# Experts' part of a gated Fourier mix as a sixth contraction chunk of the closing Strassen step

## Chip, cores, metric

One core of a Trainium2 chip runs the whole kernel in one launch. The metric is device time in microseconds, the median of the runs shown; lower is better. A profile comes from one further execution of the same program, with its own time. PE is TensorE, DVE VectorE, ACT ScalarE, POOL GpSimd; SP is the sync engine, whose queue issues most DMAs.

## What is computed

For 2048 tokens of width 640, with x, all in float32:

```python
g = sigmoid((x * gate_w).sum(-1, keepdims=True))
a = Re(DFT_seq(DFT_hidden(x)))          # as products with cos/sin matrices, 2048x2048 and 640x640
# PEER experts: 32 heads, two sets of 16 keys, top 2 of each, top 2 of their 4 sums, 256 experts
act = gelu(einsum("nd,nhkd->nhk", x, u[top_e]))
b = einsum("nhk,nhk,nhkd->nd", softmax(top_s), act, v[top_e])
out = g * a + (1 - g) * b
```

Since there are only 256 experts, b is computed densely: f[e, t] is the sum of the gates that token t gives to expert e, and the expert part is z^T v with z[e, t] = gelu(u x)[e, t] * f[e, t] * (1 - g[t]).

## The kernel before

**Precision.** Every float32 matmul is three fp32r matmuls: each operand is split into a high half (ACT copies it to fp32r, line 123) and a low half (the difference, line 124, on POOL or DVE), and `mm3` (lines 128 to 130) adds high-high, high-low and low-high into one PSUM bank. Nearly every operand passes through this chain: a DMA on SP's queue, ACT's copy, POOL's or DVE's difference, three matmuls on PE.

**Stages.** 128 "pieces" (`seq_piece`, five mm3 each, one per 128 output rows) multiply x with the sequence matrices; in between, background work is spread by a credit pump (`bg`): keys and scores, top-2 picks on DVE, and from about 400 us on the `experts` generator, which builds one-hot tables on DVE (L639), multiplies them in bursts of 64x64 matmuls (L650, 16 per table), masks the PSUM result on ACT (L609) and sums it on DVE (L615) into f. The result of the pieces, multiplied by g (L193), is stored to DRAM as the tiles pd[w, c][k]: real or imaginary part w, 512 tokens c, and 128 of the 640 hidden rows k.

**Last part.** `step(m)` forms, for each half b of the tokens, out^T = D_re^T pd[0] + D_im^T pd[1] + v^T z as 2x2 blocks: block rows of the left operand are the half's two token quarters, block columns the real and imaginary part, and the right operand's block columns are output rows 0 to 255 and 256 to 511. Strassen's method (Winograd's form) does this with seven products, the units a11, a12, s1, s2, s4, s3, a22, each over KD = 5 chunks k of 128 hidden rows. A step in a11, a12, s1 and a22 is three mm3 (two output tiles and the fifth output tile "W", rows 512 to 639, which is done plainly), in s2, s4 and s3 two. The operands s1 to s4 are sums of a11 to a22: for half 0 they are made in an earlier stage and stored (pqs), for half 1 they are summed on DVE (L800). The right operand's sums lie in TS (made by `make_sums` and `split_sums`, L738 to L742), its plain blocks in DD.

**Experts in the last part.** `load_z` (L860 to L866) loads for one quarter g, the activations and the gate sums f (four 128x128 DMAs for each of two chunks of 128 experts); `split_z` makes 1 - g (L876), multiplies twice (L879, L880) and splits into `zop`. `z_group` then multiplies with v, outside Strassen: at the end of a12 and the start of a22 (six mm3 each), at the end of s4 and behind s3 (`quarter`, four each), 20 mm3 for each half. At the very end, `very_last` holds back the second output tile's five mm3 of a22 so that the first one can be stored meanwhile.

**Order.** `at(n, f)` queues f behind piece or step n (step m counts as NPC + m, NPC = 128); loads come some steps ahead, the split of step m + 5 is emitted in step m, and each engine works through its own queue strictly in that order, waiting on semaphores. Buffers come from tags: `take` hands a raw tile to a load, `give` returns it once its split is emitted, and SP's queue stands still when the tile at its head is not free. Splits go through a ring of six (four WS, two WP).

Of the kernel before, what the change touches and what calls it, by code (L numbers as in the profile page):

```python
# [16 lines left out]
P = 128  # L17
# [19 lines left out]
NSTEP = 7 * KD  # L37
# [54 lines left out]
def gated_mix_kernel(ctx: ExitStack, tc: tile.TileContext, xT, xn, dreT, dimT, wsre, wsim, wq, kT, uT, vv, gw, out):  # L92
# [43 lines left out]
    gdr = dram.tile([S], F32, name="gdr")  # L136
# [11 lines left out]
    zc, gt, gc = (const.tile([P, 32], F32, name=t) for t in ("zc", "gt", "gc"))  # L148
    nc.gpsimd.memset(zc, 0.0)
# [246 lines left out]
    def gate():  # L396
        nc.scalar.activation(gt, zc, AF.Sigmoid)
        nc.vector.transpose(gc, gt)

    def store_gate():  # L400
        for j in range(4):
            nc.scalar.dma_start(gdr.rearrange("(i j p) -> j i p", j=4, p=32)[j], gc[32 * j:32 * j + NT])
# [191 lines left out]
    HOT = []  # L594

    def experts():
# [45 lines left out]
        def use(group):  # L642
            while masked or unmasked:
                yield settle(True)
            for i, (g, c, s) in enumerate(group):
                t = bank((6, 7, 5)[i], (P, 8, E * 4))
                pt, qt = (HOT[s // 2][:, s % 2, n].rearrange("p (m c) -> p m c", m=16) for n in range(2))
                for m in range(16):
                    r = slice(64 * (m % 2), 64 * (m % 2) + 64)
                    nc.tensor.matmul(t[r, m // 2, :], pt[:, m], qt[:, m], start=True, stop=True)  # L650
                unmasked.append((g, c, t))
                free_sets.append(s)
            yield 0.0
# [24 lines left out]
        assert not last_part  # L678
# [45 lines left out]
    def t_sum(k, n, a):  # L724

        if n < 2:
            return TS[k][:, (2 * n + a) * 2 * P:][:, :2 * P]
        if n == 2:
            return TS[5 + k // 2][:, (2 * (k % 2) + a) * 2 * P:][:, :2 * P]
        return DD[:, 0, a, k, 2 * P:4 * P] if n == 3 else TS[k][:, PAIR + a * P:][:, :P]  # L730

    def make_sums(k):
        if k == 0:
            T["t"] = big.tile([P, 9 * P], F32, name="tf", tag="xl")
# [10 lines left out]
    def split_sums(k):  # L745
        for n in [k] + ([5 + k // 2] if k % 2 == 0 else []):
# [7 lines left out]
    def load_v():  # L754
        T["f"] = big.tile([P, 2, D], F32, name="dt", tag="xf")
        nc.sync.dma_start(T["f"], vv.rearrange("k p d -> p k d"))

    def split_v():
# [7 lines left out]
    def v_neg(a):  # L766
        return TS[5 + a][:, PAIR:].rearrange("p (k d) -> p k d", k=2)
# [5 lines left out]
    at(NPC - 3, load_v)  # L773
    at(NPC, split_v)
    at(NPC + 28, store_gates, 1)


    fresh, raw_free, raw_tags = deque(), deque(), [("wf", 1)] * 5 + [(f"X{s}", 2) for s in range(10, 16)] + [("xf", 2)]
    raw, sp = {}, {}

    def take(key):
        if not fresh and raw_tags:
# [3 lines left out]
            else:  # L786
                r = big.tile([P, 2, TC], F32, name="ra", tag=t)
                fresh.extend(r[:, a] for a in range(2))
# [53 lines left out]
    def split_step(m):  # L842
        if m < 2 * NSTEP:
            b, (u, k) = m // NSTEP, divmod(m % NSTEP, KD)
            what = UNITS[u]
            key = (b, "s" if b and what in ("s1", "s2", "s4") else what, k)
# [3 lines left out]
            if b == 0 or what in ("a11", "a12", "a22", "s3", "s4"):  # L850
                give(key)

    zop = {}

    def load_z(b, n):
# [4 lines left out]
        nc.sync.dma_start(take((b, "g", n)), gdr[c * TC:(c + 1) * TC].partition_broadcast(P))  # L860
        for k in range(2):
            a, f = take((b, "za", k)), take((b, "zf", k))
# [6 lines left out]
    def split_z(b, n):  # L869

        if not zop:
            for k in range(2):
                zop[k] = big.tile([P, 2, TC], F32R, name="zo", tag=f"X{8 + k}")
        g = raw[b, "g", n]
        s = -1.0 if n == 0 else 1.0
        nc.vector.tensor_scalar(g, g, s, -s, op0=OP.mult, op1=OP.add)  # L876
        for k in range(2):
            a, f = raw[b, "za", k], raw[b, "zf", k]
            nc.vector.tensor_tensor(a, a, f, op=OP.mult)  # L879
            nc.vector.tensor_tensor(a, a, g, op=OP.mult)  # L880
            split(a, zop[k][:, 0], zop[k][:, 1], nc.gpsimd)
            give((b, "za", k))
            give((b, "zf", k))
        give((b, "g", n))
        bg.credit -= 3.5
# [19 lines left out]
    def post(b, what):  # L905
# [15 lines left out]
        elif what == "q":  # L921
            add("c22", "Y", OP.subtract)
# [5 lines left out]
    def z_group(o, c0, w, first=False, last=False, more=False):  # L928

        for k in range(2):  # L930
            h, l = zop[k][:, 0], zop[k][:, 1]
            for d in range(2):
                c = slice((c0 + d) * P, (c0 + d + 1) * P)
                mm3(roles[o][d], T["xh"][:, k, c], T["xl"][:, k, c], h, l, first and k == 0, last and k == 1, more)
                run_bg(0.68)
            if w:
                mm3(roles["W"], w(0)[:, k], w(1)[:, k], h, l, False, last and k == 1)
                run_bg(0.68)

    held = []  # L940

    def step(m):
        b, (u, k) = m // NSTEP, divmod(m % NSTEP, KD)
        what = UNITS[u]
        if k == 0:
# [8 lines left out]
            if what == "a22":  # L954
                z_group("Z", 0, v_neg, first=True)
        split_step(m + AHEAD)
        o, w, w5 = {
            "a11": ("X", lambda a: DD[:, 0, a, k, 0:2 * P], lambda a: DD[:, 0, a, k, 4 * P:]),
            "a12": ("Z", lambda a: DD[:, 1, a, k, 0:2 * P], lambda a: DD[:, 1, a, k, 4 * P:]),
            "s1": ("Y", lambda a: t_sum(k, 0, a), lambda a: DD[:, 0, a, k, 4 * P:]),  # L960
            "s2": ("X", lambda a: t_sum(k, 1, a), None),
            "s4": ("Y", lambda a: DD[:, 1, a, k, 2 * P:4 * P], None),
# [4 lines left out]
        end = k == KD - 1  # L967
        very_last = b == 1 and what == "a22"
        for d in range(1 if very_last else 2):
            c = slice(d * P, (d + 1) * P)  # L970
            mm3(roles[o][d], w(0)[:, c], w(1)[:, c], h, l, k == 0 and what in ("a11", "a12", "s1"),
                end and what not in ("a12", "s4"), more)
# [3 lines left out]
        if w5:  # L976
            mm3(roles["W"], w5(0), w5(1), h, l, k == 0 and what in ("a11", "s1"), end and what == "a22")
# [11 lines left out]
        if what == "s3":  # L989
            at(NPC + m, post, b, what)  # L990
            at(NPC + m, quarter, b)
        elif not very_last:
            at(NPC + m + 1, post, b, what)
        else:
            for d in range(2):
                if d == 1:
                    for n, x in enumerate(held):
                        mm3(roles["Z"][1], *x, False, n == KD - 1)
                for a in range(d + 1):
                    r = slice(a * TC // 2, (a + 1) * TC // 2) if d else slice(0, TC)  # L1000
                    nc.vector.tensor_tensor(res["c"][:, d, r], res["c"][:, d, r], roles["Z"][d][:, r], op=OP.subtract)
                    (nc.scalar if a else nc.sync).dma_start(out[d][:, 3 * TC + r.start:3 * TC + r.stop],
# [108 lines left out]
```

## Time and profile before

| | |
|---|---|
| time, median of 3 runs | 765.99 us (765.96 to 766.72) |
| profiled execution's own time | 766.93 us |
| its span, first to last instruction | 765.1 us |
| PE busy / matmuls | 760.0 us (99%) / 4085 |
| DVE, POOL, ACT busy | 554.7 (73%), 335.8 (44%), 307.8 us (40%) |
| granted PE clock | full throughout |

The page's slices give each engine's busy share over time; the chain of waits follows the last instruction back to what released it; the timeline has single instructions with start, length and, in brackets, the idle time before them and who ended it. A matmul's length there contains its way through the array, so consecutive matmuls overlap in the table; what a matmul costs in a stream is the distance from its start to the next one's.

### The profile page before, as it was taken

How to read it: one execution, taken by the hardware profiler on the slowest of the kernel's cores; microseconds unless marked ns; L12 is line 12 of the kernel's file. 1: busy time of each engine (PE TensorE's matmuls, PEld its weight loads, DVE VectorE, ACT ScalarE, POOL GpSimd, SP SyncE). 2: the span in 40 equal slices, each digit the busy share in tenths (PEclk: the TensorE clock that was granted, in tenths of full speed). 3: DMA queues.
4: the chain of work that ended last, by engine and by line, in shares of the span. 5: the costliest groups of instructions: out<-in, count | busy, mean ns of one | idle time of the engine just before them, and what ended most of it. 6: DMA issues, size and time to landing. Idle time of an engine off the chain costs nothing.

```text
span 765.1 us, 11062 instructions
## 1 busy us (share of the span) xinstructions
PE 760.0 (99%) x4085; PEld 620.9 (81%) x4085; DVE 554.7 (73%) x637; ACT 307.8 (40%) x548; POOL 335.8 (44%) x233
## 2 busy tenths in 40 slices
PE   9999999999999999999999999999999999999997
PEld 7777777888888888888888888888888878888886
DVE  6853151589899799999799899579978772437561
ACT  4424123221234442623522774533544553423350
POOL 5533235142242323432158674443456584549270
PEclk9999999999999999999999999999999999999999
DMA  9888696321222322310535352568864696766421
GB/s 337 340 316 302 249 378 208 111 75 42 76 62 74 107 97 63 123 51 21 170 125 167 117 157 75 174 185 286 264 236 166 208 319 219 246 194 196 124 83 69
DMA packets 73718, 130.33 MB, mean 170 GB/s; under 512 B 15168, under 2 KB 22464, under 8 KB 73408
## 3 DMA queue, kind: packets, MB, share of 16 engines
q1 hardware_dynamic: 63424, 113.23, 45.0%
q10 hardware_dynamic: 10240, 16.40, 5.9%
q8 instruction: 32, 0.52, 0.3%
q14 instruction: 22, 0.18, 0.1%
HBM read 102.84 MB, written 25.17 MB: 167 GB/s over the span
## 4 chain that ended last, share of the span: by engine, by line
PE 94%; POOL 2%; issue 2%; DMA 1%; ACT 1%; DVE 1%; DVEq 0%; POOLq 0%
PE b L128 30%; PE b L129 29%; PE b L130 29%; PE b L333 2%; PE b L215 2%; POOL WS L124 1%; PE b L650 1%; DMA ra<-pqs 1%; POOL WP L124 1%; DMA wf<-in_wsre 0%; ACT ts L123 0%; POOL ts L124 0%; DVE ts L124 0%; ACT b L609 0%; DVE tf L738 0%
## 5 line engine op out<-in xcount | busy, mean ns | idle before, releaser
L124 POOL TENSOR_TENSOR WS<-wf,WS 128x512 fp32r<-128x512 f32 x127 | 193.7, 1527 | 257.7 <-ACT WS L123 255.6
L128 PE MATMUL b<-WS,X 128*128 128x512 f32 x620 | 243.3, 392 | 0.0
L129 PE MATMUL b<-WS,X 128*128 128x512 f32 x620 | 241.4, 389 | 0.0
L130 PE MATMUL b<-WS,X 128*128 128x512 f32 x620 | 241.3, 389 | 0.0
L128 PEld LDWEIGHTS b<-WS,X 128*128 128x128 f32 x620 | 116.3, 188 | 28.3 <-issue 4.1
L130 PEld LDWEIGHTS b<-WS,X 128*128 128x128 f32 x620 | 116.4, 188 | 24.3
L129 PEld LDWEIGHTS b<-WS,X 128*128 128x128 f32 x620 | 116.4, 188 | 23.6
L123 ACT ACTIVATE WS<-wf 128x512 fp32r<-128x512 f32 x127 | 79.7, 628 | 106.6 <-PE b L130 62.8
L639 DVE TENSOR_TENSOR hot<-rows,wtab 128x1024 f16<-128x1024 f16 x64 | 59.7, 958 | 15.6 <-PE b L650 15.5
L128 PE MATMUL b<-WU,xh 128*128 128x512 f32 x160 | 62.3, 390 | 0.0
L129 PE MATMUL b<-WU,xh 128*128 128x512 f32 x160 | 62.3, 390 | 0.0
L130 PE MATMUL b<-WU,xl 128*128 128x512 f32 x160 | 62.2, 389 | 0.0
L435 ACT ACTIVATE sc<-b 128x512 f32<-128x512 f32 x32 | 19.8, 618 | 104.7 <-PE b L130 104.7
L124 POOL TENSOR_TENSOR xl<-xf,xh 128x640 fp32r<-128x640 f32 x16 | 26.0, 1630 | 79.9 <-ACT xh L123 79.9
L449 DVE TENSOR_REDUCE mm<-sc 128x64 f32<-128x1024 f32 x32 | 38.9, 1216 | 24.5 <-ACT sc L435 23.9
L124 POOL TENSOR_TENSOR WS<-ra,WS 128x512 fp32r<-128x512 f32 x32 | 45.2, 1436 | 25.9 <-ACT WS L123 25.9
L609 ACT ACTIVATE b<-b,mask 128x128 f32<-128x128 f32 x128 | 43.2, 343 | 21.1 <-PE b L650 15.6
L451 DVE TENSOR_TENSOR eq<-sc,mm 128x1024 f16<-128x1024 f32 x32 | 49.2, 1538 | 1.1
L124 POOL TENSOR_TENSOR WP<-ra,WP 128x512 fp32r<-128x512 f32 x18 | 28.0, 1564 | 29.9 <-ACT WP L123 29.7
L193 DVE SCALAR_TENSOR_TENSOR ST<-ST,grow 128x512 f32<-128x512 f32 x40 | 33.7, 904 | 9.6 <-ACT ST L222 9.6
L455 DVE TENSOR_REDUCE rr<-eq 128x64 f16<-128x1024 f16 x32 | 39.0, 1220 | 1.1
L639 DVE TENSOR_TENSOR hot<-hot,rows 128x1024 f16<-128x1024 f16 x32 | 39.0, 1219 | 0.0
(157 smaller groups left out, 1206.7 us busy)
## 6 DMA issues: line engine op xcount, KB each, us to landing
wq<-in_wq SPq DMA_DIRECT2D x32, 640.0 KB, 6.5
wf<-in_wsim SPq DMA_DIRECT2D x64, 256.0 KB, 4.0
wf<-in_wsre SPq DMA_DIRECT2D x63, 256.0 KB, 4.7
ra<-pd SPq DMA_DIRECT2D x50, 256.0 KB, 3.8
pd<-ST ACTq DMA_DIRECT2D x35, 256.0 KB, 4.7
xf<-in_xT SPq DMA_DIRECT2D x16, 320.0 KB, 3.3
ra<-pqs SPq DMA_DIRECT2D x20, 256.0 KB, 4.1
xr<-in_xn SPq DMA_DIRECT2D x15, 320.0 KB, 6.9
```

What stands on the lines that cost most here:

```text
L123: nc.scalar.activation(h, f, AF.Copy)
L124: eng.tensor_sub(l, f, h.bitcast(F32))
L128: nc.tensor.matmul(o, wh, ah, start=first, stop=False, skip_group_check=more)
L129: nc.tensor.matmul(o, wh, al, start=False, stop=False, skip_group_check=more)
L130: nc.tensor.matmul(o, wl, ah, start=False, stop=last, skip_group_check=more)
L193: nc.vector.scalar_tensor_tensor(f, f, -1.0 if w else 1.0, g, op0=OP.mult, op1=OP.mult)
L435: nc.scalar.activation(scs[i].rearrange("p h e -> p (h e)")[:, c], ps, AF.Copy)
L449: nc.vector.tensor_reduce(m, sc, op=OP.max, axis=AX.X)
L451: nc.vector.tensor_tensor(eq, sc, m[:, :, None].to_broadcast([P, HH, E]), op=OP.is_equal)
L455: nc.vector.tensor_reduce(r, eq, op=OP.max, axis=AX.X)
L609: nc.scalar.activation(f[:, :, n], f[:, :, n], AF.Copy, scale=mask4[:, n:n + 1])
L639: nc.vector.tensor_tensor(o, a, b, op=op)
```

## The change

z and v become chunk k = 5 (KD) of the same seven products: the contraction index goes from 5 to KZ = 6 chunks, so a11, a12, a21, a22 of that chunk are z of the first and second quarter for the first and second 128 experts, its right operand is v, and the sums are made of z (`sum_z`, L887 and L888 in the new numbering) and of v (`make_sums(KD)`, `split_sums(KD)`). `z_group`, `quarter`, `zop` and the negated copies of v go. With it move:

- 1 - g is made once and stored behind g (two more instructions' worth of work at piece 14); `load_z` reads it, and reads f with one 128x4x128 DMA instead of four. The first quarter's loads come at piece NPC - 6 instead of NPC - 1, the second's at step 1 instead of 21.
- `make_z` multiplies; for the first chunk of the first quarter of half 0 on POOL, four pieces before the last part, else on DVE. The split of z is the normal one of its step.
- v is loaded at NPC - 6 into another slot (X9) and split at NPC - 4, then summed at NPC - 3.
- The experts' work must be emitted before the last part (`used`); the last burst of L650 so comes behind the last piece.
- The held-back mm3 of the second tile are six now, and done in two column ranges, first 384 columns, then 128, each with its own subtraction and store.

```diff
-NSTEP = 7 * KD
+KZ = KD + 1
+NSTEP = 7 * KZ
...
-        nc.scalar.activation(gt, zc, AF.Sigmoid)
+        nc.scalar.activation(gt[:, :NT], zc, AF.Sigmoid)
+        nc.vector.tensor_scalar(gt[:, NT:], gt[:, :NT], -1.0, 1.0, op0=OP.mult, op1=OP.add)
...
     def split_v():
...
-        split(T["f"], T["xh"], T["xl"], nc.vector)
-        for a, t in enumerate(("xh", "xl")):
-            nc.scalar.activation(v_neg(a), T[t][:, :, 4 * P:], AF.Copy, scale=-1.0)
+        for w in range(2):
+            split(T[KD][:, w], T["xh"][:, w], T["xl"][:, w], nc.vector)
...
-    at(NPC - 3, load_v)
-    at(NPC, split_v)
-    at(NPC + 28, store_gates, 1)
+    at(NPC - 4, split_v)
+    at(NPC - 3, make_sums, KD)
+    at(NPC + 3, split_sums, KD)
+    at(NPC + 14, store_gates, 1)
...
-            for i in range(4):
-                i8 = (4 * c + i) % 8
-                nc.sync.dma_start(f[:, i * P:(i + 1) * P],
-                                  gd[b][i8 // 4, i8 % 4].rearrange("e f m -> (e f) m")[k * P:(k + 1) * P])
+            nc.sync.dma_start(f.rearrange("p (t m) -> p t m", t=4),
+                              gd[b][n].rearrange("t e f m -> (e f) t m")[k * P:(k + 1) * P])
...
+    def make_z(b, n, k, eng):
+
+        a, f = raw[b, f"a{n + 1}{k + 1}", KD], raw[b, "zf", 2 * n + k]
+        eng.tensor_tensor(a, a, f, op=OP.mult)
+        eng.tensor_tensor(a, a, raw[b, "g", n], op=OP.mult)
+        give((b, "zf", 2 * n + k))
...
+    def sum_z(b):
+        s, a21 = take((b, "s", KD)), raw.pop((b, "a21", KD))
+        nc.vector.tensor_add(s, a21, raw[b, "a22", KD])
+        nc.vector.tensor_add(a21, a21, raw[b, "a11", KD])
+        raw[b, "s3", KD] = a21
...
-        if what == "a12":
-            z_group("Z", 0, lambda a: T[("xh", "xl")[a]][:, :, 4 * P:], last=True)
-        if what == "s4":
-            z_group("Y", 2, None, last=True, more=True)
...
-            at(NPC + m, quarter, b)
...
-            for d in range(2):
+            for d, r, eng in ((0, slice(0, TC), nc.sync), (1, slice(0, 3 * P), nc.scalar), (1, slice(3 * P, TC), nc.sync)):
                 if d == 1:
-                    for n, x in enumerate(held):
-                        mm3(roles["Z"][1], *x, False, n == KD - 1)
-                for a in range(d + 1):
...
+                    for n, (wh, wl, h, l) in enumerate(held):
+                        mm3(roles["Z"][1][:, r], wh, wl, h[:, r], l[:, r], n == 0, n == KD)
+                nc.vector.tensor_tensor(res["c"][:, d, r], res["c"][:, d, r], roles["Z"][d][:, r], op=OP.subtract)
+                eng.dma_start(out[d][:, 3 * TC + r.start:3 * TC + r.stop], res["c"][:, d, r])
...
-        for n, i in ((0, -1), (1, 21)):
-            at(M + i, load_z, b, n)
-            at(M + i + 4, split_z, b, n)
+        at(M + 1, load_z, b, 1)
+        for i, n, k in ((-3 if b else -4, 0, 0), (-2 if b else 1, 0, 1), (6, 1, 0), (8, 1, 1)):
+            at(M + i, make_z, b, n, k, nc.gpsimd if i == -4 else nc.vector)
+        at(M + 9, sum_z, b)
...
+    bg.drain(lambda: len(used) == 32)
+    last_part, bg.credit = True, 0.0
```

The order of instructions moves at three places that matter below. First DVE's queue at the end of the pieces, before; `hot` are the one-hot tables of the last burst, L615 the sums of earlier bursts, L193 the last piece result times g, and vxl the low half of v.

```order
L639 TENSOR_TENSOR hot_3189<-rows_1124,wtab_156 128x1024
L615 TENSOR_REDUCE cd<-b_5156 128x8x16
L639 TENSOR_TENSOR hot_3189<-rows_1124,wtab_156 128x1024
L639 TENSOR_TENSOR hot_3189<-hot_3189,rows_1124 128x1024
L615 TENSOR_REDUCE cd<-b_5324 128x8x16
L615 TENSOR_REDUCE cd<-b_5341 128x8x16
L193 SCALAR_TENSOR_TENSOR ST<-ST,grow 128x512 x5
L124 TENSOR_TENSOR vxl<-dt,vxh 128x1280
L876 TENSOR_SCALAR ra<-ra 128x512
L879 TENSOR_TENSOR ra<-ra 128x512
```

The same stretch in the changed kernel, whose line numbers are higher by one or two here:

```order
L641 TENSOR_TENSOR hot_3189<-rows_1124,wtab_155 128x1024
L617 TENSOR_REDUCE cd<-b_5156 128x8x16
L125 TENSOR_TENSOR vxl<-dt,vxh 128x640 x2
L641 TENSOR_TENSOR hot_3189<-rows_1124,wtab_155 128x1024
L641 TENSOR_TENSOR hot_3189<-hot_3189,rows_1124 128x1024
L745 TENSOR_TENSOR tf<-dt 128x512
L746 SCALAR_TENSOR_TENSOR tf<-tf,dt 128x256
L747 TENSOR_TENSOR tf<-tf 128x256
L748 TENSOR_TENSOR tf<-dt 128x256
L749 TENSOR_TENSOR tf<-dt 128x128
L194 SCALAR_TENSOR_TENSOR ST<-ST,grow 128x512 x5
L617 TENSOR_REDUCE cd<-b_5371 128x8x16
```

The split of v stands ahead of the last two table instructions now, and its sums (L745 to L749) ahead of the products with g.

Second POOL's queue around the last split of a piece (the last row with wf), before:

```order
L124 TENSOR_TENSOR WS<-wf,WS 128x512
L124 TENSOR_TENSOR WP<-ra,WP 128x512 x2
L124 TENSOR_TENSOR WS<-ra,WS 128x512 x4
L124 TENSOR_TENSOR WP<-ra,WP 128x512 x2
L124 TENSOR_TENSOR WS<-ra,WS 128x512
L124 TENSOR_TENSOR zo<-ra,zo 128x512 x2
L124 TENSOR_TENSOR WS<-ra,WS 128x512 x3
```

And in the changed kernel:

```order
L125 TENSOR_TENSOR WS<-wf,WS 128x512
L878 TENSOR_TENSOR ra<-ra 128x512
L879 TENSOR_TENSOR ra<-ra 128x512
L125 TENSOR_TENSOR WP<-ra,WP 128x512 x2
L125 TENSOR_TENSOR WS<-ra,WS 128x512 x4
L125 TENSOR_TENSOR WP<-ra,WP 128x512 x2
L125 TENSOR_TENSOR WS<-ra,WS 128x512
L125 TENSOR_TENSOR ts<-tf,ts 128x256 x2
L125 TENSOR_TENSOR WS<-ra,WS 128x512 x3
```

The two products of `make_z` come ahead of the first split of the last part, and two smaller splits of v's sums take the place of the two of z.

Third PE's queue at its end, before (the last mm3 of the held-back tile):

```order
L128 MATMUL b_6380<-WS,ts 128x512
L129 MATMUL b_6380<-WS,ts 128x512
L130 MATMUL b_6380<-WS,ts 128x512
L128 MATMUL b_6380<-WS,ts 128x512
L129 MATMUL b_6380<-WS,ts 128x512
L130 MATMUL b_6380<-WS,ts 128x512
```

And in the changed kernel, where the step from the first to the second column range is seen:

```order
L129 MATMUL b_6379<-WS,ts 128x384
L130 MATMUL b_6379<-WS,ts 128x384
L131 MATMUL b_6379<-WS,ts 128x384
L129 MATMUL b_6379<-WP,ts 128x128
L130 MATMUL b_6379<-WP,ts 128x128
L131 MATMUL b_6379<-WP,ts 128x128
```

Fifteen matmuls of 512 columns have become 18 of 384 and 18 of 128.

More of the change, by code (lines that the diff above doesn't have):

```diff
@@ L926, in post @@
             put(b, 1, 0, res["c"])
-    def z_group(o, c0, w, first=False, last=False, more=False):
-        for k in range(2):
-            h, l = zop[k][:, 0], zop[k][:, 1]
-            for d in range(2):
[L933 to L938, printed above, removed]
     held = []
     def step(m):
-        b, (u, k) = m // NSTEP, divmod(m % NSTEP, KD)
+        b, (u, k) = m // NSTEP, divmod(m % NSTEP, KZ)
         what = UNITS[u]
@@ L966, in step @@
         more = what in ("s2", "s3", "s4")
-        end = k == KD - 1
+        end = k == KD
         very_last = b == 1 and what == "a22"
@@ L970, in step @@
             c = slice(d * P, (d + 1) * P)
-            mm3(roles[o][d], w(0)[:, c], w(1)[:, c], h, l, k == 0 and what in ("a11", "a12", "s1"),
-                end and what not in ("a12", "s4"), more)
+            mm3(roles[o][d], w(0)[:, c], w(1)[:, c], h, l, k == 0 and what in ("a11", "a12", "s1", "a22"), end, more)
             run_bg(0.68)
@@ L976, in step @@
         if w5:
-            mm3(roles["W"], w5(0), w5(1), h, l, k == 0 and what in ("a11", "s1"), end and what == "a22")
+            mm3(roles["W"], w5(0), w5(1), h, l, k == 0 and what in ("a11", "s1"),
+                end and what in ("a12", "a22"))
             run_bg(0.68)
```

138 lines of the change are left out of this document (63 added, 75 removed).

## Prediction

> **What bounds the kernel now.** The page comes first: its busy times, then the chain of what ended last.
>
> ```profile
> PE 760.0 (99%) x4085; PEld 620.9 (81%) x4085; DVE 554.7 (73%) x637; ACT 307.8 (40%) x548; POOL 335.8 (44%) x233
> PE 94%; POOL 2%; issue 2%; DMA 1%; ACT 1%; DVE 1%; DVEq 0%; POOLq 0%
> ```
>
> PE is never out of work, and no other engine is close. Its matmuls are pipelined, though, so the price of one must come from the distance of two starts, in PE's timeline: the program's last matmuls, and neighbours of 256 columns from the expert activations; the last row is the group of their weight loads.
>
> ```profile
> 760.59 0.39 PE L129 MATMUL b<-WS,ts 128*128 128x512 f32 x1
> 760.82 0.39 PE L130 MATMUL b<-WS,ts 128*128 128x512 f32 x1
> 148.32 0.28 PE L129 MATMUL b<-xl,WU 128*128 128x256 f32 x1
> 148.44 0.28 PE L130 MATMUL b<-xh,WU 128*128 128x256 f32 x1
> L129 PEld LDWEIGHTS b<-xl,WU 128*128 128x128 f32 x80 | 15.3, 192 | 0.3
> ```
>
> A 512-column matmul costs 0.227 us (three make 0.68), a 256-column one 0.120 us: 0.107 us for 256 columns more, and 0.013 us that doesn't depend on them. The last part is such a stream. It starts at 610.68 and has 660 matmuls, 149.6 us at 0.227; PE's last one starts at 760.82, so the stream itself would end it at 760.1, and 0.7 us are stalls. They stand in two places of the timeline:
>
> ```profile
> 610.68 0.39 PE L128 MATMUL b<-WP,DD 128*128 128x512 f32 x1
> 611.14 0.39 PE L130 MATMUL b<-WP,DD 128*128 128x512 f32 x1
> 611.43 0.50 PE L128 MATMUL b<-WP,DD 128*128 128x512 f32 x1
> 611.76 0.40 PE L129 MATMUL b<-WP,DD 128*128 128x512 f32 x1
> 629.24 0.39 PE L128 MATMUL b<-WS,DD 128*128 128x512 f32 x1
> 629.90 0.50 PE L129 MATMUL b<-WS,DD 128*128 128x512 f32 x1 [0.27 <-POOL WS L124]
> 630.24 0.40 PE L130 MATMUL b<-WS,DD 128*128 128x512 f32 x1
> ```
>
> Beyond 0.227 each, the gaps lose 0.06 and 0.11 us at 611 and 0.43 and 0.11 us at 630: 0.7 in all. So the kernel is bound by the number and width of its matmuls; a change pays by what it takes from PE, as long as the operands still come in time.
>
> **Fewer matmuls.** z and v were these groups by line and form (L129 and L130 have as many):
>
> ```profile
> L128 PE MATMUL b<-zo,vxh 128*128 128x512 f32 x36 | 14.0, 389 | 0.0
> L128 PE MATMUL b<-zo,ts 128*128 128x512 f32 x4 | 1.6, 389 | 0.0
> ```
>
> That is 40 mm3, 20 for each half. As a sixth chunk they cost one step of each unit: 3+3+3+2+2+2+3 = 18. Four mm3 fewer are 12 matmuls, 12 x 0.227 = **-2.72 us**.
>
> **The cut tail.** Of the matmuls that stay, 18 of 512 columns become 18 of 384 and 18 of 128. By the two distances above, 384 columns cost 0.013 + 384 x 0.107/256 = 0.173 us. No row shows 128 columns. The straight line gives 0.067 us and is the lower bound; the 512-column matmul's 0.227 is the upper one, should a narrow fp32r matmul lose its speed altogether. I take the nearest row, 0.120 us at 256 columns, because each matmul also brings its own load of 128 weights, which doesn't shrink with the columns: its record at 256 columns is 192 ns long (the row with PEld above), longer than the distance of two matmuls there. The 18 pairs then cost 18 x (0.173 + 0.120 - 0.227) = **+1.20 us**; 0.24 at the lower bound, 3.12 at the upper.
>
> The Trainium skill, page "TensorE: Matmul & The Clock Gate", bears on this choice. Its section "LDWEIGHTS (loading the stationary operand)" gives a weight load as columns / 1.2 ns, an estimate of 107 ns for 128 columns whatever moves; the section "Back-to-back issue gap" gives an isolated matmul N / 2.4 + 2.5 ns, an estimate of 56 ns for 128. By the first the sum keeps about +1.2 us, by the second it would have about +0.1. The trace agrees with either at 256 and 512 columns and shows nothing below.
>
> **After the last matmul.** The two halves' subtractions run one after the other, then a store:
>
> ```profile
> 761.24 0.75 DVE L1001 TENSOR_TENSOR ST<-ST,b 128x256 f32<-128x256 f32 x2 [3.39 <-PE b L130]
> 762.03 0.35 ACTq L1002 DMA_DIRECT2D out_y<-ST  x1
> L1001 DVE TENSOR_TENSOR ST<-ST,b 128x512 f32<-128x512 f32 x1 | 0.7, 687 | 9.5 <-PE b L130 9.5
> L1001 DVE TENSOR_TENSOR ST<-ST,b 128x256 f32<-128x256 f32 x2 | 0.8, 418 | 3.4 <-PE b L130 3.4
> ```
>
> Now only a 128-column one follows: 418 - (687 - 418)/2 = 284 ns instead of 0.75 us, **-0.47 us**. The 384-column one runs while PE does the 18 narrow matmuls (1.2 us even at the lower bound; it takes about 0.55 us), so it and its store are covered. The last matmul's own way to its end falls from 0.39 us by 0.053 for each 128 columns, to 0.23: **-0.16 us**. The store's fixed rest (from 762.4 to 765.1) I keep; it is half as large, for which I count nothing.
>
> **The stalls.** At 611 PE waited for ACT to empty the piece's banks; ACT had the masks of the burst (its 32 matmuls, in PE's timeline, come first here) in front:
>
> ```profile
> 606.52 0.69 PE L650 MATMUL b<-hot 128*64 128x64 f16 x32
> 607.01 2.85 ACT L609 ACTIVATE b<-b,mask 128x128 f32<-128x128 f32 x8 [4.94 <-PE b L650]
> 610.29 2.54 ACT L222 ACTIVATE ST<-b 128x512 f32<-128x512 f32 x5
> ```
>
> The masks now stand behind L222, which can follow each bank from 607 on. At 630 PE waited for a split that POOL began late, since ACT's queue stood behind the copies of z, which waited for DVE:
>
> ```profile
> 613.43 6.05 POOL L124 TENSOR_TENSOR WS<-ra,WS 128x512 fp32r<-128x512 f32 x3 [1.66 <-ACT WS L123]
> 624.89 1.67 DVE L880 TENSOR_TENSOR ra<-ra 128x512 f32<-128x512 f32 x1
> 627.30 1.29 POOL L124 TENSOR_TENSOR zo<-ra,zo 128x512 fp32r<-128x512 f32 x1 [1.29 <-ACT zo L123]
> ```
>
> Those copies are gone, and the first z is made on POOL before the part starts. Adding POOL's queue at its slowest, 2.0 us a split (three took 6.05 us from 613.43), from 611 on behind L222, steps 6 to 11 are ready from 619 to 631, and PE, at 9 x 0.227 = 2.04 us a step from 610.6, wants them from 622.8 to 633: 2 to 4 us in hand. So **-0.7 us**; at worst nothing.
>
> **What moves and is covered.** `make_z` on POOL is two products with the shape of a split, at most 2.0 us each. There is a gap for them:
>
> ```profile
> 599.72 1.69 POOL L124 TENSOR_TENSOR WS<-wf,WS 128x512 fp32r<-128x512 f32 x1 [1.09 <-ACT WS L123]
> 601.62 3.19 POOL L124 TENSOR_TENSOR WP<-ra,WP 128x512 fp32r<-128x512 f32 x2 [0.21 <-ACT WP L123]
> 610.48 1.29 POOL L124 TENSOR_TENSOR WS<-ra,WS 128x512 fp32r<-128x512 f32 x1 [5.67 <-ACT WS L123]
> ```
>
> The 5.7 us idle take the 4.0; without the gap steps 0 and 1 would be late one for one. The loads of v and of the first quarter move into the emptiest stretch of the DMA engines, the second quarter's into a full one:
>
> ```profile
> 590.00:600.00 10.00, 10.00 (x46) 8.27 (x45) 8.55 (x14) 6.85 (x20) 6.56 (x7) 1.00 0.24 58
> 620.00:630.00 10.00, 9.73 (x44) 7.75 (x42) 6.49 (x4) 4.39 (x9) 8.71 (x7) 1.00 0.96 344
> ```
>
> On SP's queue the second quarter (1.3 MB) now stands ahead of s1's five loads (1.3 MB), behind the last piece's stores, which wait for DVE's products with g:
>
> ```profile
> 610.92 4.91 DVE L193 SCALAR_TENSOR_TENSOR ST<-ST,grow 128x512 f32<-128x512 f32 x5 [0.34 <-ACT ST L222]
> ```
>
> DVE reaches v's five sums at about 608 (next part); if each took as long as the slowest L639 there, 1.8 us, the stores would leave by 608 + 9 + 4.9 = 622. 2.6 MB at 344 GB/s take 7.6 us, to 629.5; s1's first split, 2.6 us on ACT and POOL, is due for PE's step 12, at 635. The z of the second quarter and its sums, six DVE instructions of at most 1.8 us, end by 641 and are wanted for step 17, at 645. The second half's loads have slots freed many steps ahead. `1 - g` costs one small DVE instruction at piece 14, beside matmuls.
>
> **A new wait.** The last burst's 32 matmuls come at about 609.8 now, 15 matmuls later than 606.4, and PE's queue behind them is the whole last part. DVE must have the tables by then, with v's split ahead of them. DVE before:
>
> ```profile
> 602.48 1.18 DVE L639 TENSOR_TENSOR hot<-rows,wtab 128x1024 f16<-128x1024 f16 x1
> 603.58 1.77 DVE L639 TENSOR_TENSOR hot<-hot,rows 128x1024 f16<-128x1024 f16 x1
> 615.75 2.58 DVE L124 TENSOR_TENSOR vxl<-dt,vxh 128x1280 fp32r<-128x1280 f32 x1
> 599.57 0.68 DVE L639 TENSOR_TENSOR hot<-hot,rows 128x1024 f16<-128x1024 f16 x1
> 599.55 1.45 ACT L609 ACTIVATE b<-b,mask 128x128 f32<-128x128 f32 x4
> 614.25 1.31 ACT L123 ACTIVATE vxh<-dt 128x1280 fp32r<-128x1280 f32 x1
> 592.41 1.41 POOL L124 TENSOR_TENSOR WS<-wf,WS 128x512 fp32r<-128x512 f32 x1
> dt<-in_vv SPq DMA_DIRECT2D x1, 640.0 KB, 4.0
> ```
>
> v's split takes the place of the first L639: 602.5 + 2.6 + 1.1 + 1.8 = 608.0, 1.8 us in hand. ACT's two copies of v fit before, from 601.0 for 1.3 us. v's load stands on SP behind one into a slot that POOL frees at 593.8 (its split at 592.41), and lands 4 us later.
>
> **The sum.** -2.72 + 1.20 - 0.47 - 0.16 - 0.7 = -2.85 us against the profiled execution's 766.93 (765.1 span): 764.1. That execution lies 0.9 us above the median of 765.99, so the forecast is **763.1 us**.
>
> **The rivals.**
> - *Narrow matmuls at the straight line*, 0.067 us: 0.96 us better, 762.2. For it: 256 to 512 is a straight line through almost no fixed part. Against: weight loads can't get shorter. [...]
> - *Narrow matmuls at full price*, 0.227 us: 1.92 us worse, 765.1, no change that can be told. Nothing in the trace speaks for it but that no row excludes it.
> - *DVE late at the burst* (the slower side). DVE's two-input instructions stretch while POOL works: L639 took 1.77 us beside POOL's WP splits, and one at 599.57 only 0.68. POOL now works without a pause from 601.6 to about 608, over just these four. If each waits out a whole POOL instruction (2.0 us), they end 4 x 2.0 - 1.6 (the excess already in the rows) = 6.4 us later, at 614.4; PE stands for 4.6 us, and 763.1 becomes 767.7, slower. It costs PE nothing up to 1.8 us of lateness, then one for one; past 4.7 us the gain is gone. Against: the durations summed are already those beside a busy POOL.
> - *Stalls stay or come elsewhere*, 0.7 to 2 us: 763.8 to 765.8.
>
> The page "SBUF — State Buffer", section "Who interferes with whom", of the Trainium skill says that a DVE instruction with two SBUF inputs and a GpSimd one that reads SBUF lock each other out for a whole instruction, whichever starts first. By that rule the third rival is the mechanism to fear; the trace agrees that such instructions stretch (0.68 to 1.77 us).
>
> **Chances.** Forecast 0.50, straight line 0.17, full price 0.13, DVE late 0.10, other stalls 0.10. About 0.2% (1.5 us) is what a measurement of this kernel can tell from no change. Faster by that, below 764.5: the first two and a part of the stalls, 0.70. Within: full price, the rest of the stalls and a mild DVE delay, 0.20. Slower: 0.10. The range runs from the straight line, 762.0, to 766.5, which takes in full price with stalls kept (765.8) and leaves out the worst of the third rival.
>
> **What would show it.** Right: 12 x 512-column equivalents fewer; narrow matmuls 0.12 us apart; no gap above 0.24 us between 610 and the end; the last DVE instruction about 0.3 us. Wrong: a gap ahead of the burst with DVE's tables as releaser; POOL or ACT named as releaser of PE after 610; narrow matmuls 0.2 us apart; SP's queue standing at the second quarter's loads so that s1 comes late.

## The result: 0.3% faster, two thirds of the forecast gain

| | median, us | ratio to the kernel before, 95% interval |
|---|---|---|
| kernel before | 766.04 | |
| changed kernel | 764.11 | 0.9973 [0.9963, 0.9983] |
| changed kernel, second measurement (e1_again) | 764.04 | 0.9969 [0.9957, 0.998] |

The change takes off 1.9 us where 2.85 were forecast; 764.1 lies inside the range of 762.0 to 766.5. One execution of the first measurement, the one in which its profile was taken, ran for 1277 us at a granted clock of 0.557, so the changed kernel's lines are from the profile of the second one, e1_again (763.66 us, span 761.8).

Its page has the same two lines that opened the prediction, busy times and the chain of what ended last:

```profile
PE 757.1 (99%) x4091; PEld 620.0 (81%) x4091; DVE 573.3 (75%) x649; ACT 313.8 (41%) x558; POOL 342.3 (45%) x238
PE 99%; DMA 0%; DVE 0%; ACT 0%; issue 0%
```

PE still bounds the kernel. It has six matmuls more, as forecast (12 fewer, and 18 that were cut in two), and is busy 2.9 us less; DVE has 18.6 us more work, which the chain doesn't show. The end of the program on PE (start, length, then in brackets an idle time and its releaser), with what follows on DVE and SP's queue:

```profile
754.23 0.33 PE L130 MATMUL b<-WS,ts 128*128 128x384 f32 x1
...
755.45 0.34 PE L131 MATMUL b<-WS,ts 128*128 128x384 f32 x1
756.43 0.33 PE L129 MATMUL b<-WP,ts 128*128 128x128 f32 x1 [0.65 <-DVE ST L983]
756.59 0.28 PE L130 MATMUL b<-WP,ts 128*128 128x128 f32 x1
756.71 0.28 PE L131 MATMUL b<-WP,ts 128*128 128x128 f32 x1
...
758.38 0.27 PE L131 MATMUL b<-WS,ts 128*128 128x128 f32 x1
755.82 0.55 DVE L983 TENSOR_TENSOR ST<-ST,b 128x384 f32<-128x384 f32 x1 [3.14 <-PE b L131]
758.69 0.29 DVE L983 TENSOR_TENSOR ST<-ST,b 128x128 f32<-128x128 f32 x1 [2.32 <-PE b L131]
759.04 0.34 SPq L984 DMA_DIRECT2D out_y<-ST  x1
```

The 384-column matmuls stand 0.174 us apart (seven distances from 754.23 to 755.45), the 128-column ones 0.111 (fifteen from 756.71 to 758.38). Between the two ranges PE stands still: 0.98 us from start to start, of which 0.81 are lost. DVE reads the first range from 755.82 to 756.37, and the first narrow matmul, which writes other columns of the same PSUM bank, starts at 756.43, 0.06 us after DVE is done. PE's waits from 600 us to the end are this one row (total, times, longest):

```profile
PE b L129 <- DVE ST L983: 0.6, 1, 0.6
```

Nor are any two starts between 609.88 and 755.45 more than 0.24 us apart. So the two stalls of before, at 611 and 630, are gone, and one that the prediction did not have is there.

**The ledger**, from the distances of PE's starts in the two profiles:

| step of the prediction | forecast, us | in the trace, us |
|---|---|---|
| Fewer matmuls | -2.72 | -2.72 (the 512-column distance is 0.227 as before) |
| The cut tail | +1.20 | +1.90 = 18 x (0.174 + 0.111 - 0.227) + 0.81 + 0.05 |
| The stalls | -0.7 | -0.7 |
| After the last matmul | -0.63 | -0.74 |
| sum | -2.85 | -2.26 |

The +0.05 is the first narrow matmul, 0.16 us from the next. The last line of the table compares 4.28 us from the last matmul's start to the span's end (765.1 - 760.82) with 3.42 (761.8 - 758.38), each less the last distance, which the stream's sum has already. The profiles differ by 3.27 us (766.93 to 763.66), 1.0 more than the ledger: that is the start of the program, told at the end. The two measurements, -1.9 and, repeated, -2.2 us (766.26 to 764.04), lie near the ledger's sum.

### The profile page after: what moved, and what is told of

It is laid out like the page before. It is cut to its first block, busy times and chain, and to the rows that moved or that the text cites. A ratio compares the mean times of both kernels' runs of the same rounds, so it can differ in the third digit from the quotient of the medians.

```text
span 1275.3 us, 11081 instructions
## 1 busy us (share of the span) xinstructions
PE 1270.7 (100%) x4091; PEld 737.1 (58%) x4091; DVE 510.9 (40%) x649; ACT 316.5 (25%) x558; POOL 317.1 (25%) x238
## 4 chain that ended last, share of the span: by engine, by line
PE 100%; DVE 0%; issue 0%
PE b L129 31%; PE b L131 31%; PE b L130 31%; PE b L334 2%; PE b L216 2%; PE b L653 1%; PE b L284 0%; DVE ST L983 0%
## 5 line engine op out<-in xcount | busy, mean ns | idle before, releaser
L129 PE MATMUL b<-WS,X 128*128 128x512 f32 x620 | 357.5, 577 | 0.0
L130 PE MATMUL b<-WS,X 128*128 128x512 f32 x620 | 356.7, 575 | 0.0
L131 PE MATMUL b<-WS,X 128*128 128x512 f32 x620 | 356.6, 575 | 0.0
L125 POOL TENSOR_TENSOR WS<-wf,WS 128x512 fp32r<-128x512 f32 x127 | 177.9, 1401 | 595.8 <-ACT WS L124 586.7
L129 PEld LDWEIGHTS b<-WS,X 128*128 128x128 f32 x620 | 133.1, 215 | 109.1 <-issue 67.3
L130 PEld LDWEIGHTS b<-WS,X 128*128 128x128 f32 x620 | 135.8, 219 | 101.0 <-issue 61.4
L131 PEld LDWEIGHTS b<-WS,X 128*128 128x128 f32 x620 | 135.8, 219 | 100.4 <-issue 57.2
L641 DVE TENSOR_TENSOR hot<-rows,wtab 128x1024 f16<-128x1024 f16 x64 | 50.6, 816 | 163.7 <-PE b L653 163.7
L130 PE MATMUL b<-WU,xh 128*128 128x512 f32 x160 | 92.4, 578 | 0.0
L129 PE MATMUL b<-WU,xh 128*128 128x512 f32 x160 | 92.1, 576 | 0.0
L131 PE MATMUL b<-WU,xl 128*128 128x512 f32 x160 | 92.0, 575 | 0.0
L125 POOL TENSOR_TENSOR WS<-ra,WS 128x512 fp32r<-128x512 f32 x39 | 51.1, 1312 | 77.7 <-ACT WS L124 75.9
L124 ACT ACTIVATE WS<-ra 128x512 fp32r<-128x512 f32 x55 | 34.5, 631 | 110.0 <-PE b L131 103.4
L130 PEld LDWEIGHTS b<-WU,xh 128*128 128x128 f32 x160 | 35.7, 223 | 25.3 <-issue 15.0
L129 PEld LDWEIGHTS b<-WU,xh 128*128 128x128 f32 x160 | 35.7, 223 | 25.2 <-issue 14.6
L131 PEld LDWEIGHTS b<-WU,xl 128*128 128x128 f32 x160 | 35.0, 219 | 25.5 <-issue 14.2
```

The lines of the kernel that those rows point to most:

```text
L124: nc.scalar.activation(h, f, AF.Copy)
L125: eng.tensor_sub(l, f, h.bitcast(F32))
L129: nc.tensor.matmul(o, wh, ah, start=first, stop=False, skip_group_check=more)
L130: nc.tensor.matmul(o, wh, al, start=False, stop=False, skip_group_check=more)
L131: nc.tensor.matmul(o, wl, ah, start=False, stop=last, skip_group_check=more)
L641: nc.vector.tensor_tensor(o, a, b, op=op)
```

## Experiments

Theory: the missing 0.7 us are PE's wait for DVE at the change of range, because both ranges lie in one bank, while narrow matmuls, stalls and DVE's tables are as forecast. Rivals: the whole cut costs more than forecast because narrow matmuls are slow; or the gain was smaller elsewhere (z on POOL, the stalls), and the wait at the end only takes the place of another.

The results of all runs; the last column is the time from the last part's first matmul to the span's end in the profile, which leaves out what happens before the part. Each ratio is against the kernel before as measured beside that run: 766.26 us for e1 to e3, 766.17 for e4 to e7, 766.16 for e8.

| kernel | median, us | ratio, 95% interval | last part to end, us |
|---|---|---|---|
| before, again (e7) | 766.11 | 0.9998 [0.9988, 1.0008] | 154.45 |
| changed, again (e1) | 764.04 | 0.9969 [0.9957, 0.998] | 152.27 |
| one range (e2) | 763.44 | 0.9962 [0.9948, 0.9975] | 151.39 |
| 256 and 256, one bank (e3) | 763.20 | 0.9962 [0.9949, 0.9974] | 151.73 |
| 384 and 128, two banks (e4) | 762.97 | 0.9957 [0.9943, 0.997] | 151.36 |
| 256 and 256, two banks (e5) | 762.84 | 0.9956 [0.9943, 0.9968] | 150.96 |
| first z on DVE (e6) | 765.73 | 0.9993 [0.9984, 1.0001] | 152.00 |
| before, z split later (e8) | 765.76 | 0.9994 [0.9985, 1.0003] | 153.89 |

**e1_again: the changed kernel, nothing edited.**

> The changed kernel once more, for a profile at the full PE clock. My account: 12 matmuls fewer, the 18 narrow ones 0.12 us apart, no distance over 0.24 us between two 512-column starts from the part's start to the held-back tile, last DVE instruction 0.28 us; 763.2 by that sum, while the time measured first, 764.1, asks for 0.9 us that it lacks. Rival 1: the narrow ones are 0.17 us apart (18 x 0.05 = 0.9 us). Rival 2: a stall of about 0.9 us that the sum took as gone or did not see. Rival 3: nothing in the program, but a clock granted below full for some stretch.

Measured: 764.04 us; its lines are above. The time repeats. The narrow matmuls stand 0.111 us apart, not 0.17, and the granted clock was 1.000, so it is the second rival: a stall that the sum did not see. A shorter one, 0.34 us from 609.54 to 609.88 between the part's first two matmuls, is told further down.

**e2_one_range: the held-back products in one range of 512 columns, subtracted in two halves, as before the change.**

```diff
-for d, r, eng in ((0, slice(0, TC), nc.sync), (1, slice(0, 3 * P), nc.scalar), (1, slice(3 * P, TC), nc.sync)):
+for d in range(2):
...
-            mm3(roles["Z"][1][:, r], wh, wl, h[:, r], l[:, r], n == 0, n == KD)
+            mm3(roles["Z"][1], *x, n == 0, n == KD)
```

> The changed kernel with the held-back tile in one range of 512 columns and the two halves subtracted after it, as before the change. By my sum the two ranges cost 1.20 on PE and give 0.63 back behind it, so this one is 0.57 us faster than the changed kernel. If narrow matmuls cost 0.067 us it is 0.39 us slower; if 0.227, 2.5 us faster; if 0.17, 1.5 us faster.

Measured: 763.44 us, 0.6 below e1; by the profiles, from the part's start, 0.88. The cut as the change makes it is a loss, and all the gain comes from the other edits. That the time fell by the 0.57 us expected is chance: that sum had no wait in it, and by the ledger (+1.90 - 0.74) 1.16 us had to go. The missing 0.3 us lies behind the last store's issue, from which this execution took 3.4 us to the span's end, against 3.1 for the same store in the two profiles of the kernel before; why stays open.

**e3_half_half: the ranges at 256 columns instead of 384 and 128, still in one bank.**

```diff
-(1, slice(0, 3 * P), nc.scalar), (1, slice(3 * P, TC), nc.sync)
+(1, slice(0, 2 * P), nc.scalar), (1, slice(2 * P, TC), nc.sync)
```

> The changed kernel with the held-back tile in two ranges of 256 columns. PE: 18 x (0.120 + 0.120) instead of 18 x (0.173 + 0.120) if narrow ones cost 0.12, 0.96 us less; behind it a subtraction of 418 instead of 284 ns and 0.05 more of the matmul's own way, 0.19 us more: 0.8 us faster than the changed kernel. If narrow matmuls of 128 columns cost 0.067 us: 0.2 us slower or equal. If 0.17: 1.7 us faster.

Measured: 763.20 us, 0.84 below e1 as expected, but 0.54 by the profiles from the part's start. PE's timeline at the change of range:

```profile
754.52 0.28 PE L131 MATMUL b<-WS,ts 128*128 128x256 f32 x1
755.31 0.38 PE L129 MATMUL b<-WP,ts 128*128 128x256 f32 x1 [0.51 <-DVE ST L983]
```

The matmuls stand 0.120 us apart, but the wait is there with other widths too: 0.79 us from start to start instead of 0.12, so 0.67 are lost where e1 lost 0.81. That is 0.14 less, and the subtraction of 256 columns (0.42 us) is 0.13 shorter than that of 384 (0.55). So the wait goes with DVE's read of the first range, and not with a change of width.

**e4_two_banks: 384 and 128 columns as in the change, the second range in a bank of its own.**

```diff
-for d, r, eng in ((0, slice(0, TC), nc.sync), (1, slice(0, 3 * P), nc.scalar), (1, slice(3 * P, TC), nc.sync)):
+Z = roles["Z"] + [bank(3)]
+for d, r, eng in ((0, slice(0, TC), nc.sync), (1, slice(0, 3 * P), nc.scalar), (2, slice(3 * P, TC), nc.sync)):
...
-            mm3(roles["Z"][1][:, r], wh, wl, h[:, r], l[:, r], n == 0, n == KD)
+            mm3(Z[d][:, r], wh, wl, h[:, r], l[:, r], n == 0, n == KD)
```

> The changed kernel with the second column range (128) accumulated in a PSUM bank of its own. Theory: what the sum lacked is PE's 0.98 us from the last 384-column matmul to the first 128-column one, a wait for DVE's subtraction, which reads the bank that PE is about to write. Then this one has no such distance (0.17 us there), the last matmul starts 0.8 us earlier, and the time is 0.8 us below the changed kernel's 764.0. Rival: the distance belongs to the change of width itself or to the PE queue; then nothing changes, 764.0.

Measured: 762.97 us, 1.07 below e1, and 0.91 by the profiles from the part's start. PE and DVE at the same place:

```profile
756.20 0.33 PE L131 MATMUL b<-WS,ts 128*128 128x384 f32 x1
756.38 0.22 PE L129 MATMUL b<-WP,ts 128*128 128x128 f32 x1
756.44 0.27 PE L130 MATMUL b<-WP,ts 128*128 128x128 f32 x1
756.55 0.28 PE L131 MATMUL b<-WP,ts 128*128 128x128 f32 x1
...
758.22 0.27 PE L131 MATMUL b<-WS,ts 128*128 128x128 f32 x1
756.58 0.56 DVE L985 TENSOR_TENSOR ST<-ST,b 128x384 f32<-128x384 f32 x1 [3.14 <-PE b L131]
```

The step from the first range to the second is 0.18 us, no wait of PE is left, and DVE subtracts beside the narrow matmuls, as the prediction had it. Same work, same widths, one bank more: this is the missed term, shown by taking it away. Each bank is one tile in this program, so the runs don't tell whether the wait goes by the bank or by the tile. The narrow matmuls keep their 0.111 us without the wait. What sets that distance is seen in the weight loads of the same stretch (PE's row of loads):

```profile
756.21 0.19 PEld L129 LDWEIGHTS b<-WP,ts 128*128 128x128 f32 x1
756.38 0.19 PEld L130 LDWEIGHTS b<-WP,ts 128*128 128x128 f32 x1
756.49 0.19 PEld L131 LDWEIGHTS b<-WP,ts 128*128 128x128 f32 x1
```

The first of these loads began under a matmul of 384 columns, 0.17 us ahead of the narrow matmul that it is for (756.38), and that matmul held up the next one by only 0.06 us. From there on the loads start 0.11 us apart, and each narrow matmul starts 0.06 us behind its own load (756.44, 756.55): the matmuls follow the loads. So the range of 128 columns is paced by the loads.

**e5_two_banks_256: two banks, 256 columns each.** The edit is that of e4 with `2 * P` for `3 * P`.

> Two ranges of 256 columns, each in its own bank. Against the version with two ranges of 256 in one bank (763.2) the wait of about 0.75 us is gone: 762.5. Against the one with a single range (763.4): 18 x (0.240 - 0.227) = 0.24 us more on PE, 0.33 us less in the last subtraction and 0.11 us less of the last matmul's own way: 763.2. Rival: no wait is removed, 763.2 by the first account too; the two accounts are 0.7 us apart because the second takes no difference in how fast the store ends.

Measured: 762.84 us, the lowest median of the study, and midway between the two accounts, so the time decides for neither. The profile does: the two ranges' matmuls stand 0.12 us from start to start throughout, so the wait is gone, and from the part's start it is 0.77 us shorter than e3's. What follows the last matmul:

```profile
757.16 0.28 PE L131 MATMUL b<-WS,ts 128*128 128x256 f32 x1
757.48 0.42 DVE L985 TENSOR_TENSOR ST<-ST,b 128x256 f32<-128x256 f32 x1 [1.74 <-PE b L131]
757.96 0.34 SPq L986 DMA_DIRECT2D out_y<-ST  x1
```

18 pairs of 256 columns cost 18 x 0.240 = 4.32 us on PE instead of 18 x 0.285 = 5.13 for 384 and 128; behind the last matmul it takes 3.8 us to the end (span 761.0) instead of 3.5 in e4. By the profiles it is 0.40 below e4, a difference that the times (0.13 us) don't resolve.

**e6_dve_z: the first z is multiplied on DVE, not on POOL, at the same step.**

```diff
-at(M + i, make_z, b, n, k, nc.gpsimd if i == -4 else nc.vector)
+at(M + i, make_z, b, n, k, nc.vector)
```

> The changed kernel with the first z made on DVE, not on POOL. In DVE's queue its two products and v's five sums then stand ahead of the last two table instructions. From 601.5 us that is 2.6 to 3.2 (v's split) + 2.0 to 3.5 + 2.2 to 5.9 + 1.9 to 3.6: the tables are there between 610.2 and 617.7, and PE wants them at 608.9. Theory (a late DVE at the burst stalls PE one for one): a PE wait of 1.3 to 8.8 us ahead of the burst, with DVE as releaser, and a time as much above 764.0. Rival: the time lost there is won back later, since the part then has more operands ready: no change in the time beyond 0.5 us.

Measured: 765.73 us, and nearly all of the change's gain is gone. PE's burst of L653 with its wait, then DVE's queue around the last tables:

```profile
609.81 0.44 PE L653 MATMUL b<-hot 128*64 128x64 f16 x16
611.58 0.44 PE L653 MATMUL b<-hot 128*64 128x64 f16 x16 [1.32 <-DVE hot L641]
604.92 1.77 DVE L878 TENSOR_TENSOR ra<-ra 128x512 f32<-128x512 f32 x1
606.73 1.67 DVE L879 TENSOR_TENSOR ra<-ra 128x512 f32<-128x512 f32 x1
609.71 0.42 DVE L748 TENSOR_TENSOR tf<-dt 128x256 f32<-128x256 f32 x1
610.04 0.28 DVE L749 TENSOR_TENSOR tf<-dt 128x128 f32<-128x128 f32 x1
610.24 0.68 DVE L641 TENSOR_TENSOR hot<-rows,wtab 128x1024 f16<-128x1024 f16 x1
610.85 0.68 DVE L641 TENSOR_TENSOR hot<-hot,rows 128x1024 f16<-128x1024 f16 x1
```

DVE's products push the tables to 611.5, and the second half of the burst stands 1.77 us behind the first, with the whole last part behind it: from the burst's start to the part's it takes 2.14 us instead of 0.63 in e1, and the program is 1.7 us slower. So a late table costs PE its lateness, as the prediction's third rival had it, and that is what POOL's part of the change buys off. That rival's other half, instructions that stretch beside POOL, is not what made them late here: DVE had more to do.

**e7_before_again: the kernel before, nothing edited.**

> The kernel before, unchanged, for a second profile. The two profiles of before and of the changed kernel differ by 1.0 us already in the first 20 us, where PE's full clock came at 6.6 us in the one and at 4.1 us in the other. If that is a matter of the single execution, this profile may show another time of the grant than 6.6 us, with the rest of the program shifted by as much; if it is one of the program, it shows 6.6 us again.

Measured: 766.11 us, ratio 0.9998 [0.9988, 1.0008]. The full clock was granted at 6.1 us, not 6.6, and the first of the pieces' matmuls starts earlier too, at 18.94 us instead of 19.30:

```profile
18.94 0.39 PE L128 MATMUL b<-WS,X 128*128 128x512 f32 x1
```

So the time of the grant belongs to the single execution. The stalls stand where the first profile had them, so both are the program's.

**e8_late_split: the kernel before, with the first quarter's z made and split two steps later.**

```diff
-at(M + i + 4, split_z, b, n)
+at(M + i + (6 if i < 0 and b == 0 else 4), split_z, b, n)
```

> The kernel before the change, with the first quarter's products and split of z emitted two steps later (after the split of three more tiles on ACT and POOL; DVE's and SP's order stays). Theory (the stall at 630 stands on ACT's queue behind the copies of z, which wait for DVE): ACT copies and POOL splits the three tiles while DVE still makes z, so POOL's idle 1.29 us goes and the two long starts at 629 to 630 (0.66 and 0.34 us, 0.54 us lost) are gone; the stalls at 611 (0.17 us) stay; the time falls by about 0.5 us to 765.5. Rival (POOL is simply too slow there, whatever stands ahead of it): PE still loses 0.4 to 0.6 us somewhere between 625 and 635, the time stays at 766.0. The time alone can hardly tell 0.5 us; the starts of the profile do.

Measured: 765.76 us, ratio 0.9994 [0.9985, 1.0003], as little as forecast and not to be told from before. POOL's queue and PE's starts tell it:

```profile
622.07 5.13 POOL L124 TENSOR_TENSOR WS<-ra,WS 128x512 fp32r<-128x512 f32 x3
627.17 2.54 POOL L124 TENSOR_TENSOR zo<-ra,zo 128x512 fp32r<-128x512 f32 x2
```

```profile
610.90 0.50 PE L128 MATMUL b<-WP,DD 128*128 128x512 f32 x1
611.24 0.40 PE L129 MATMUL b<-WP,DD 128*128 128x512 f32 x1
...
629.16 0.39 PE L130 MATMUL b<-WS,DD 128*128 128x512 f32 x1
629.39 0.39 PE L128 MATMUL b<-WS,DD 128*128 128x512 f32 x1
```

POOL splits three tiles while DVE still makes z, and its pause of 1.29 us ahead of the second z split is gone. The starts around 629 stand 0.23 us apart, where before the distances were 0.66 and 0.34; the stall at 611 (0.34 us from 610.90 to 611.24) stays. From the part's start the profile is 0.56 us shorter than e7's. So the stall at 630 was ACT's queue behind the copies of z, not POOL's speed.

## Why the prediction was right, and where it fell short

The range holds the measured time, but that says little, since it reaches from 762.0 us to above the kernel before. The gain came out a third smaller than the sum, nearly all of it by one step.

**Fewer matmuls** was right: PE's count is 4091, and the distance of 0.227 holds.

**The cut tail** is the step that failed. Its sum, 18 x (0.173 + 0.120 - 0.227), took the 36 narrower matmuls as one stream, and the next paragraph put DVE's subtraction of the first range beside the second range's matmuls. Both are true only if PE may write one range while DVE reads the other. In this program it waits: with one bank 0.81 us are lost, with two none (e1, e4). "No gap above 0.24 us between 610 and the end" was the sign that the prediction itself named, and it did not hold: 0.98 us from 755.45. In kind and in time (763.8 to 765.8) this is its fourth rival, stalls that come elsewhere, though it had no such place in mind. The Trainium skill states the rule that the sum left out: page "PSUM — Partial Sum Buffer", section "PSUM bank collisions raise a hardware error", says that TensorE writing and VectorE reading one bank in the same 32 partitions collide even at other columns, and asks for semaphores by bank instead of by address. The trace agrees in so far as the program has that wait, 0.65 us by its row; what the chip would do without it was not tried.

The size of a narrow matmul was nearly right: 0.111 us instead of 0.120, far from the straight line's 0.067 and from full price, so both of those rivals are out. The Trainium skill's page "TensorE: Matmul & The Clock Gate", section "LDWEIGHTS (loading the stationary operand)", gives the estimate of 107 ns already named, and the trace sides with it against the 56 ns of the formula in "Back-to-back issue gap": e4's loads stand 0.11 us apart. That section gives the formula for an isolated matmul and says that it is too low for 128 columns in a stream, for which it has about 81 ns; the trace's 0.111 us is above that too. Nor did the trace quite agree with the formula at 256 and 512 columns, as the prediction says: it gives 109 and 216 ns, and the trace 0.120 and 0.227 us. By that estimate of 107 ns the prediction's term would have been 18 x (0.173 + 0.107 - 0.227) = +0.95 us, not the "about +1.2" that it says there.

The parts of the miss, by the trace alone: +0.81 for the wait, +0.05 behind it, -0.16 for the narrower price, which is the step's 0.70.

**After the last matmul**: the last subtraction took 0.29 us, as forecast. The term of -0.16 was counted wrongly: the stream's sum had already shortened the last distance from 0.227 to 0.120, and beyond that distance the last matmul's record is 0.16 us long in both kernels (0.39 - 0.227, 0.27 - 0.111). The store made up for it, by chance: 2.76 us from its issue to the span's end (761.8 - 759.04) instead of 3.07 (765.1 - 762.03), where nothing had been counted.

**The stalls** went as forecast, both of them. e8 shows the cause of the larger one. That of the smaller, ACT's masks ahead of L222, is only argued from the order: no run takes it away alone.

**A new wait** did not come, but with half the margin. PE's burst and the part's first matmuls, and what DVE and POOL did ahead of them:

```profile
608.91 0.69 PE L653 MATMUL b<-hot 128*64 128x64 f16 x32
609.54 0.50 PE L129 MATMUL b<-WP,DD 128*128 128x512 f32 x1
609.88 0.39 PE L130 MATMUL b<-WP,DD 128*128 128x512 f32 x1
601.47 3.16 DVE L125 TENSOR_TENSOR vxl<-dt,vxh 128x640 fp32r<-128x640 f32 x2
604.55 1.77 DVE L641 TENSOR_TENSOR hot<-rows,wtab 128x1024 f16<-128x1024 f16 x1
606.24 1.78 DVE L641 TENSOR_TENSOR hot<-hot,rows 128x1024 f16<-128x1024 f16 x1
610.43 1.52 DVE L748 TENSOR_TENSOR tf<-dt 128x256 f32<-128x256 f32 x1
611.88 1.37 DVE L749 TENSOR_TENSOR tf<-dt 128x128 f32<-128x128 f32 x1
600.36 1.75 POOL L878 TENSOR_TENSOR ra<-ra 128x512 f32<-128x512 f32 x1
602.19 1.75 POOL L879 TENSOR_TENSOR ra<-ra 128x512 f32<-128x512 f32 x1
603.90 3.57 POOL L125 TENSOR_TENSOR WP<-ra,WP 128x512 fp32r<-128x512 f32 x2
```

The tables were ready at 608.0, the time that was forecast, but that is chance. This whole execution began 1.0 us earlier, which moved the burst from 609.8 to 608.9 and the start of v's split from 602.5 to 601.5; v's split and the first table then took 3.16 and 1.77 us beside POOL where the sum had 2.6 and 1.1. So DVE was 1.0 us slower than forecast, and 0.9 us were in hand, not 1.8. The 0.34 us behind the burst is no new stall; the kernel before lost the same 0.11 us behind its burst, ahead of the part. POOL's two products took 3.5 us (4.0 forecast) in the gap that had been found for them.

These rows also show how near the third rival was, and that a part of it came. Beside POOL, DVE's sums of 256 and 128 columns took 1.52 and 1.37 us, and each table 1.8; in e6, begun with POOL idle, the same instructions took 0.42, 0.28 and 0.68. Beside POOL the size hardly matters: an instruction takes about as long as POOL's (1.8 us each beside the tables, 1.4 beside the two sums, where POOL did three splits in 4.19 us). The Trainium skill's page "SBUF — State Buffer", section "Who interferes with whom", has DVE instructions with two SBUF inputs and GpSimd ones that read SBUF lock each other out for whole instructions, and the trace agrees. The worst case of the rival, a further whole POOL instruction for each of the four on top of durations measured beside POOL, did not come.

**What moves and is covered** held. s1's first tile is the one whose times the prediction had worked out. ACT's copy, POOL's split and PE's first product of it, each the first of its row:

```profile
630.21 1.29 ACT L124 ACTIVATE WP<-ra 128x512 fp32r<-128x512 f32 x2 [3.19 <-DMA ra<-pqs]
630.92 2.99 POOL L125 TENSOR_TENSOR WP<-ra,WP 128x512 fp32r<-128x512 f32 x2 [3.50 <-ACT WP L124]
634.15 0.39 PE L129 MATMUL b<-WP,ts 128*128 128x512 f32 x1
```

ACT waits 3.2 us for this load, which came late as forecast; the split's first half is done at about 632.4 (half of 2.99 us from 630.92), 1.7 us before PE wants it.

## What to carry to other kernels

When the last accumulation is cut so that a first part can be read out early, each part needs a PSUM bank of its own: in one bank PE waited 0.8 us for the reader, and the cut cost more than it brought (e1 against e2). Widths of the cut are then chosen by PE's price, which for fp32r with new weights each time hardly falls from 256 to 128 columns (0.227, 0.174, 0.120 and 0.111 us for 512, 384, 256 and 128). That speaks for the even cut, and e5's profile is 0.40 us shorter than e4's, but the medians, 762.84 and 762.97 us, don't tell the two apart. And work that is moved into a stage for the sake of fewer matmuls brings that gain only if its operands are made on an engine that has a gap ahead of PE's next need: the same two products on DVE instead of POOL made PE wait and took back nearly all of it (e6).

## What else the runs showed

The program's first 20 us vary by about a microsecond from one execution to the next, whatever the kernel. PE's first matmuls and the first one of the pieces' three, before:

```profile
4.67 2.77 PE L215 MATMUL b<-WS,X 128*128 128x512 f32 x7
19.30 0.39 PE L128 MATMUL b<-WS,X 128*128 128x512 f32 x1
```

and in the changed kernel (e1):

```profile
4.53 3.04 PE L216 MATMUL b<-WS,X 128*128 128x512 f32 x12 [0.16 <-ACT WS L254]
18.29 0.39 PE L129 MATMUL b<-WS,X 128*128 128x512 f32 x1
```

Seven matmuls in 2.77 us against twelve in 3.04. In the first of these executions the starts are 0.43 us apart from 5.27 to 6.55 us and 0.23 soon after; the trace's record of the clock has the full clock granted from 6.6 us on, so the "full throughout" of the table before the prediction holds from there. In e1 it was granted at 4.1 us, ahead of all these matmuls, and they stand 0.23 us apart from the second on. Here it is worth 1.0 us, half of the change's effect, and it is why two single profiles must not be compared by their spans alone.

The last store's way from its issue to the span's end went with its size: 2.5 to 2.8 us for 128 columns (2.8 in e1, 759.04 to 761.8, and in e4; 2.5 in e6), and 3.0 to 3.4 us for 256 (3.0 in e5, 757.96 to 761.0, and in e3; 3.1 before; 3.4 in e2), one execution each. Up to 0.4 us of scatter between executions of one size is as much as several of the differences that the profiles above are read for.
